# Grouped-query attention over a cache and a token mixer: ring loads in halves and another order of work at the layers' changes

## The chip, the cores and the metric

The kernel runs on one core of a Trainium2 chip. A core has a tensor engine (TensorE, PE in the profile, with its weight loads as PEld), a vector engine (VectorE, DVE), a scalar engine for activations (ScalarE, ACT), GpSimd (POOL) and SyncE (SP), which here issues nearly all transfers from the chip's memory to the core's SBUF. Each engine works through its own queue of instructions in order and waits on semaphores that other engines and transfers raise. Sums of matrix products gather in PSUM, in banks of 128 partitions by 512 float32.

The metric is the time of one execution on the device, in microseconds (us). Of the kernel before, three runs were taken; the number that counts is their median.

## The reference

Two layers, each a grouped-query attention block over a cache (one new token, batch of 2) and a token mixer. All is float32.

```python
B, Sq, D = 2, 1, 512
Hq, Hkv, Sk, Dh = 32, 8, 32768, 128        # 4 query heads share one K/V head
def _A_ref(x, k_cache, v_cache, wq, wo):
    q = (x @ wq).reshape(B, Sq, Hq, Dh).transpose(0, 2, 1, 3)
    ...
    scores = jnp.einsum("bhqd,bhkd->bhqk", q, k) * (Dh ** -0.5)
    p = _softmax(scores, axis=-1)
    o = jnp.einsum("bhqk,bhkd->bhqd", p, v)
    return o.transpose(0, 2, 1, 3).reshape(B, Sq, Hq * Dh) @ wo
def _B_ref(x, w1, b1, w2, b2):             # F = 1792
    h = _layernorm(x, axis=-1)
    u = _gelu(jnp.einsum("bsd,sf->bdf", h, w1) + b1)
    y = jnp.einsum("bdf,fs->bds", u, w2) + b2
    return y.transpose(0, 2, 1)
x = A_x
x = x + _A_ref(_layernorm(x), A_k_cache, A_v_cache, A_wq, A_wo)
x = x + _B_ref(_layernorm(x), B_w1, B_b1, B_w2, B_b2)
x = x + _A_ref(_layernorm(x), A_k_cache, A_v_cache, A_wq, A_wo)
x = x + _B_ref(_layernorm(x), B_w1, B_b1, B_w2, B_b2)
```

The K and V caches hold 32768 keys of 128 numbers for each of 2 x 8 pairs of batch and K/V head: 16 MB of K and 16 MB of V for a pair, read in both layers.

## The kernel before, in words

**Units and chunks.** A unit is one (layer, batch, K/V head); there are 32, numbered n in the order of the list `units` (lines 268 to 279). Each unit's K and V are read in 8 chunks of 4096 keys (c = 0 to 7), 2 MB each. In SBUF a chunk fills one *cell* of `mem`: 128 partitions of 16 KB (line 102). There are 13 cells and a rest. A K chunk is used in two parts of 8 tensor-engine products each (`k_chunk`, line 413, with 128 x 512 results in a PSUM tile `scores`; four chunks share one bank, so a unit has two "halves" of scores), a V chunk in two parts of 8 products (`v_chunk`, line 553, into the PSUM tile `acc`). Part 0 reads the first half of the cell, part 1 the second.

**Softmax of a unit.** `max_1` and `max_2` (lines 427 to 440) make the maxima over all scores, with one small product each; `turn_scores` transposes a half of the scores from PSUM into the SBUF tile S[0] or S[1]; ScalarE makes the exponentials, either head by head (`exponentials`, line 448) or, at the changes, a whole half after one vector operation (`exponentials_at_once`, lines 460 and 463). `denominators`, `out_0`, `out_1`, `out_2` turn the sums of V into the block's output rows (the tile `rows`, line 236).

**The order.** There is no scheduler: the chunks of all units stand in one list, `stream`, sorted by the keys of lines 845 to 855. For each entry the program emits its loads (`load_k`, `load_v`), then its products; everything else is hung onto points of this list by `at(time, function)` and emitted when that many chunks (or half chunks) have been emitted. So the times in the code are positions in each engine's queue, not clock times. V of unit n is interleaved with K of unit n + 1.

**Loads.** SyncE issues the loads in the order of the list; a load waits until the cell it fills has been read by the tensor engine. The transfers of one queue then run one after another. `spread` (line 163) chooses where a chunk of the ring goes: into a whole cell, if one is found with at least two cells of loads between its release and its use, or into two halves of cells, each loaded by itself (`half`, line 147).

**The changes of layer.** Most heads are run for both batches before the first layer ends; three heads are kept for the change (`RESIDENT`), and head 7 is the `keeper`: of its K, chunks 0, 1 and 2 stay in cells 0, 1 and 9 (`KEPT_K`), of its V chunks 1 to 7 (nearly all) in other cells (`KEPT`), from the unit of layer 0 to that of layer 1. There are two such changes, one for each batch: N1 = 13 (unit (0, 0, 7), the last of layer 0, batch 0) and N2 = 16 (unit (0, 1, 7)). Because so much is kept, the ring of free cells is short there: the cells 7 and 8, that is four halves.

At the change after unit n = N1 the following runs (the same at N2, with other numbers):

- V of unit 13 ends (time 226, `vend`). `out_0` to `out_2` and `take_rows` make its output row; `mix_1` and `mix_2` (line 639) bring it into a PSUM tile `bcast` and take its mean and deviation.
- Meanwhile K chunks 2 to 7 of unit 14 = (0, 1, 5) are run (chunks 0 and 1 were run earlier).
- `hidden_sum` (time 228) is the token mixer: 14 pairs of a gelu on ScalarE (line 778) and a multiply-add on VectorE (lines 793, 795). `mix_3` (time 230.5, between the two parts of chunk 6) sums it with one product (line 803), copies it (line 805, ScalarE) and takes statistics; `to_columns` (time 231, line 302) brings the row into columns and writes xnT, the next layer's normalised input (lines 305 and 307).
- `make_q` for unit 15 = (1, 0, 7): steps 0 and 1 are the four query products (line 338, two tensor-engine passes each), emitted between the parts of K chunk 7 (time 231.5); step 2 copies the query row (line 347), step 3 transposes it (line 351).
- The maxima of unit 14 at time 232 and 232.5, on both sides of part 0 of K chunk 0 of unit 15 (kept in its cell); exponentials at 232.5 and 233.
- From time 233 V chunks of unit 14 and K chunks of unit 15 alternate. Of these K chunks 0, 1 and 2 are resident and need no load.

Before the change of layer the maximum over a half of the scores is emitted right with the last product of that half (line 423).

## Time and profile before

| | us |
|---|---|
| runs | 2508.97, 2509.38, 2503.17 |
| median of the runs | 2508.97 |
| profiled execution, its own time | 2503.93 |
| span of that execution's instructions | 2502.1 |
| tensor engine busy with products | 1386.8 (55% of the span) |
| VectorE busy | 239.8 (10%) |
| ScalarE busy | 187.9 (8%) |
| mean granted clock of the tensor engine | 0.767 |

The profile is of one execution. Its page lists busy times by engine, the span in 40 equal slices (with the data rate of each slice and the granted clock of the tensor engine), the DMA queues, the chain of waits that ended last, and groups of like instructions. Other views used below: the timeline (start, duration, engine, line, operation, tiles, count; in brackets the idle time before it and what ended it), the instructions in windows of time (for each engine the busy time and the count, then the granted clock, DMA share and GB/s), and the instructions of one source line with the time from a load's issue to its landing. SPq is SyncE's queue, which issues the loads (line 136). Lines 413 and 553 are the products of K and V, with 8 of them to half a chunk.

### The profile page before, as it was taken

How to read it: one execution, taken by the hardware profiler on the slowest of the kernel's cores; microseconds unless marked ns; L12 is line 12 of the kernel's file. 1: busy time of each engine (PE TensorE's matmuls, PEld its weight loads, DVE VectorE, ACT ScalarE, POOL GpSimd, SP SyncE). 2: the span in 40 equal slices, each digit the busy share in tenths (PEclk: the TensorE clock that was granted, in tenths of full speed). 3: DMA queues.
4: the chain of work that ended last, by engine and by line, in shares of the span. 5: the costliest groups of instructions: out<-in, count | busy, mean ns of one | idle time of the engine just before them, and what ended most of it. 6: DMA issues, size and time to landing. Idle time of an engine off the chain costs nothing.

```text
span 2502.1 us, 20483 instructions
## 1 busy us (share of the span) xinstructions
PE 1386.8 (55%) x9270; PEld 372.1 (15%) x9270; DVE 239.8 (10%) x632; ACT 187.9 (8%) x554; POOL 4.9 (0%) x17
## 2 busy tenths in 40 slices
PE   4545554645445554667577675455546555456546
PEld 1111111111111111111121121111111111111112
DVE  0000000000000000004013110000000000010002
ACT  0000000000000000002012010000000000011002
POOL 0000000000000000000000000000000000000000
PEclk8777777877777777878797887777777777777778
DMA  9999999999999999999999999999999999999996
GB/s 419 435 433 432 432 432 432 433 436 428 434 429 432 433 427 435 429 425 372 427 427 399 409 427 436 432 434 433 432 433 429 433 432 433 433 432 428 434 433 287
DMA packets 33072, 1063.04 MB, mean 425 GB/s; under 512 B 3925, under 2 KB 3929, under 8 KB 4826
## 3 DMA queue, kind: packets, MB, share of 16 engines
q1 hardware_dynamic: 32696, 1061.70, 98.8%
q8 instruction: 73, 1.20, 0.2%
q14 instruction: 13, 0.11, 0.0%
q10 hardware_dynamic: 290, 0.04, 0.0%
HBM read 1061.72 MB, written 0.00 MB: 424 GB/s over the span
## 4 chain that ended last, share of the span: by engine, by line
DMA 73%; PE 25%; DVE 1%; issue 1%; ACT 0%; SPq 0%; POOL 0%; DVEq 0%; ACTq 0%
DMA mem<-in_v_dram 37%; DMA mem<-in_kt_dram 36%; PE scores L413 11%; PE acc L553 10%; PE kept L338 1%; DVE acc L795 1%; PE rows L236 1%; PE bcast L338 0%; PE small L437 0%; PE small L593 0%; PE small L584 0%; PE bcast L803 0%; PE kept L735 0%; PE small L431 0%; PE small L351 0%
## 5 line engine op out<-in xcount | busy, mean ns | idle before, releaser
L413 PE MATMUL scores<-mem,small_sb 128*32 128x512 f32 x4096 | 638.3, 740 | 610.0 <-DMA mem<-in_kt_dram 609.7
L553 PE MATMUL acc<-mem,S 128*16 128x512 f32 x4088 | 611.2, 736 | 455.0 <-DMA mem<-in_v_dram 453.7
L413 PEld LDWEIGHTS scores<-mem,small_sb 128*32 128x32 f32 x4096 | 149.4, 128 | 999.5 <-issue 889.8
L448 ACT ACTIVATE S<-S,small_sb 128x128 f32<-128x128 f32 x240 | 123.6, 519 | 2112.4 <-DVE small_sb L439 1644.8
L553 PEld LDWEIGHTS acc<-mem,S 128*16 128x16 f32 x4088 | 134.2, 110 | 826.3 <-issue 692.5
L423 DVE TENSOR_REDUCE small_sb<-scores 128x1 f32<-128x512 f32 x64 | 44.2, 691 | 915.5 <-PE scores L413 915.5
L443 DVE STREAM_TRANSPOSE S<-scores 128x512 f32<-128x512 f32 x64 | 45.4, 710 | 130.1 <-PE acc L553 130.1
L338 PE MATMUL kept<-mem,small_sb 128*2 128x512 f32 x104 | 51.0, 616 | 1.7 <-DVE small_sb L264 1.7
L236 PE MATMUL rows<-mem,small_sb 128*1 128x512 f32 (+1 forms) x276 | 48.8, 612 | 2.6 <-ACT mem L778 2.4
L448 ACT ACTIVATION_READ_ACCUMULATOR S<-S,small_sb 128x1 f32 x240 | 44.8, 187 | 0.0
L433 DVE TENSOR_REDUCE small_sb<-small 1x4 f32<-1x128 f32 x32 | 8.9, 279 | 277.8 <-PE small L431 277.8
L523 DVE SCALAR_TENSOR_TENSOR S<-acc,small_sb,S 128x128 f32<-128x128 f32 x93 | 32.6, 351 | 3.3
L586 DVE RECIPROCAL small_sb<-small 128x4 f32<-128x4 f32 x32 | 5.9, 184 | 281.8 <-PE small L584 281.8
L595 DVE TENSOR_TENSOR small_sb<-small,small_sb 128x4 f32<-128x4 f32 x31 | 5.1, 164 | 288.2 <-PE small L593 288.2
L778 ACT ACTIVATE S<-bcast,small_sb 128x512 f32<-128x512 f32 x28 | 21.5, 776 | 98.9 <-DVE small_sb L647 96.7
L351 PE MATMUL small<-small_sb,mem 2*128 2x2 f32 x112 | 14.8, 250 | 17.9 <-DVE mem L347 17.9
L521 DVE TENSOR_SCALAR S<-acc,small_sb 128x128 f32<-128x128 f32 x31 | 10.8, 348 | 112.9 <-PE acc L553 112.9
L593 PEld LDWEIGHTS small<-small_sb,S 128*128 128x128 f32 x62 | 12.2, 248 | 46.6 <-issue 41.5
L338 PE MATMUL bcast<-mem,small_sb 128*1 128x512 f32 (+1 forms) x40 | 18.5, 592 | 0.0
L795 DVE SCALAR_TENSOR_TENSOR acc<-S,small_sb,acc 128x512 f32<-128x512 f32 x24 | 18.1, 755 | 2.5
L351 PEld LDWEIGHTS small<-small_sb,mem 2*128 2x128 f32 x112 | 13.7, 188 | 30.5 <-DVE mem L347 27.3
L431 PE MATMUL small<-small_sb 128*1 128x128 f32 x64 | 16.7, 355 | 0.6 <-DVE small_sb L429 0.6
(134 smaller groups left out, 267.8 us busy)
## 6 DMA issues: line engine op xcount, KB each, us to landing
mem<-in_kt_dram SPq DMA_DIRECT2D x35, 2048.0 KB, 17.6
mem<-in_v_dram SPq DMA_DIRECT2D x27, 2048.0 KB, 21.4
mem<-in_v_dram SPq DMA_DIRECT2D x9, 4096.0 KB, 27.1
mem<-in_wqo_dram SPq DMA_DIRECT2D x14, 2048.0 KB, 33.2
mem<-in_kt_dram SPq DMA_DIRECT2D x7, 4096.0 KB, 24.1
mem<-in_kt_dram SPq DMA_DIRECT2D x18, 1024.0 KB, 7.6
mem<-in_v_dram SPq DMA_DIRECT2D x13, 1024.0 KB, 7.0
mem<-in_v_dram SPq DMA_DIRECT2D x2, 1280.0 KB, 26.5
```

Of the source, the lines that this page charges most:

```text
L236: nc.tensor.matmul(rows[32 * g : 32 * g + b + 1, :], weights if b else weights[:, 1:], row, start=False, stop=True, skip_group_check=True,)
L338: nc.tensor.matmul(q_ps[n][:m, :], xnT[:, d, b : b + m], wq_at(h)[:, d, :], start=(d == 0), stop=(d == DT - 1),)
L351: nc.tensor.matmul(pt[:, r * m : (r + 1) * m], q_row[n][:m, r * DH : (r + 1) * DH], ident[:m, :m], start=True, stop=True,)
L413: nc.tensor.matmul(sc_ps[n, half][32 * g : 32 * g + 32, :], q, kc[k * NG + g], start=(i == 0 and k == 0), stop=(i == PACK - 1 and k == SUB ...
L423: nc.vector.tensor_reduce(mx[n][:, half : half + 1], sc_ps[n, half], axis=AX.X, op=ALU.max)
L431: nc.tensor.matmul(pm[:1, :P], mxa, ident, start=True, stop=True)
L443: nc.vector.transpose(S[half], sc_ps[n, half])
L448: nc.scalar.activation(s[:, :, h], s[:, :, h], AF.Exp, bias=neg[n][:, h : h + 1], scale=SCALE, accum_out=lsum[n][:, half, h : h + 1],)
L523: nc.vector.scalar_tensor_tensor(t, acc[:, k * DH : (k + 1) * DH], mask[:, k : k + 1], t, op0=ALU.mult, op1=ALU.add)
L553: nc.tensor.matmul(acc[32 * g : 32 * g + R * QT, :], S[half][:, col : col + R * QT], vc[q], start=(c == 0 and q < NG), stop=(c == NCH - 1 ...
L778: nc.scalar.activation(hid[key, f], px[key], AF.Gelu_apprx_tanh, bias=shift[key][:, f : f + 1], scale=slope[key][:, f : f + 1],)
L795: nc.vector.scalar_tensor_tensor(h if f == FT - 1 else acc, h, w, acc, op0=ALU.mult, op1=ALU.add)
```

## The change

No operation is added to or removed from the computation. The edits:

- `spread` takes `parted`: K chunks 2 to 7 of the units N1 + 1 and N2 + 1 are always loaded as two halves, where chunks 2 and 3 had gone into whole cells.
- At the two changes `mix_2` moves from time vend + 1.5 to vend + 1 and `hidden_sum` from vend + 2 to vend + 1, so that both stand ahead of K chunk 3 of the unit (the chunk at vend + 1); `mix_3` from vend + 4.5 to vend + 5 (behind K chunk 6, no longer between its parts), `to_columns` from vend + 5 to vend + 5.5 (between the parts of K chunk 7). The maximum over the first half of that unit's scores becomes a function of its own, `highest`, and is emitted at vend + 4.5, behind the sum's work in VectorE's queue, no longer with K chunk 3.
- The query products become `q_products`: one product ahead of `max_1`, one between `max_1` and `max_2`, two behind the first exponentials; all at `kend` = vend + 6, ahead of V chunk 0. They had stood between the parts of K chunk 7.
- In `stream` the V chunks of the units N1 + 1 and N2 + 1 get keys two lower: V chunks 0 and 1 come first, then K chunk 0 of the next unit, then they alternate. So V ends two places earlier against K, and K chunks 0, 1 and 2, which are resident, each stand two V chunks later.
- What follows from the positions: in the ring of four halves (7.5, 8, 8.5, 7, in cells) now go K chunks 2 to 7 and V chunks 0 to 4 of the unit, where it had been K chunks 4 to 7 and V chunks 0 to 2 (at the second change some of the V halves go to cell 0). K chunk 3 of the next unit and all that follows are in whole cells as before; K chunk 6 of unit 19 is one whole cell, where it had been two halves.
- Unit 15's (and 18's) K ends one place later and its V begins where it did, so `max_2`, both halves of exponentials and V chunk 0 stand together, where K chunk 1 of unit 16 had stood between the maxima and V chunk 0.

```diff
--- before.py
+++ after.py
@@ -160,10 +160,10 @@
 
         return sum(brings[int(-(-a // 1)) : b])
 
-    def spread(until):
+    def spread(until, parted=False):
 
         k = min((*range(WCELL0 + 1), KEPT[3][1]), key=lambda k: (-fit(k, 1, until), idle(k)))
-        if fit(k, 1, until) >= 2:
+        if fit(k, 1, until) >= 2 and not parted:
             hold(k, 1, until)
             return [cells(k)]
         return [half(until - 0.5), half(until)]
@@ -320,6 +320,21 @@
         layer, b, h = unit_of(n)
         return units.index((layer, B - 1, h)) if b == 0 and (layer == 0 or h in passing) else None
 
+    def q_products(n, *ds):
+
+        layer, b, h = unit_of(n)
+        m = 1 if partner(n) is None else B
+        for d in ds:
+            if d == 0:
+                q_ps[n] = pfix.tile([P, 512], F32, name="bcast") if N1 < n <= N3 + 2 else kept[0]
+            nc.tensor.matmul(
+                q_ps[n][:m, :],
+                xnT[:, d, b : b + m],
+                wq_at(h)[:, d, :],
+                start=(d == 0),
+                stop=(d == DT - 1),
+            )
+
     def make_q(n, step, place=None):
 
 
@@ -330,18 +345,8 @@
             if step == 3:
                 nc.vector.tensor_copy(qpad[n % 2][:, 28 : 28 + R], q_kept.pop(n))
             return
-        if step == 0:
-
-            q_ps[n] = pfix.tile([P, 512], F32, name="bcast") if N1 < n <= N3 + 2 else kept[0]
         if step < 2:
-            for d in range(step * DT // 2, (step + 1) * DT // 2):
-                nc.tensor.matmul(
-                    q_ps[n][:m, :],
-                    xnT[:, d, b : b + m],
-                    wq_at(h)[:, d, :],
-                    start=(d == 0),
-                    stop=(d == DT - 1),
-                )
+            q_products(n, 2 * step, 2 * step + 1)
         if step == 2:
             q_row[n] = spot() if place is None else place
             nc.vector.tensor_copy(q_row[n][:m, :], q_ps[n][:m, :])
@@ -388,7 +393,7 @@
             hold(own, m, until)
             bufs = [cells(own, m)]
         elif limit == RING:
-            bufs = spread(until)
+            bufs = spread(until, n in (N1 + 1, N2 + 1) and c > 1)
         else:
             bufs = [buffer(m, limit, until)]
         src, f = piece(kt, b * HKV + h, c, m), 0
@@ -420,7 +425,12 @@
         if i == PACK - 1 and part == SUB - 1:
             if half == 0:
                 mx[n] = field(n, 0, HALVES)
-            nc.vector.tensor_reduce(mx[n][:, half : half + 1], sc_ps[n, half], axis=AX.X, op=ALU.max)
+            if half or n not in (N1 + 1, N2 + 1):
+                highest(n, half)
+
+    def highest(n, half):
+
+        nc.vector.tensor_reduce(mx[n][:, half : half + 1], sc_ps[n, half], axis=AX.X, op=ALU.max)
 
     m4, neg = {}, {}
 
@@ -848,7 +858,7 @@
             if n in (N1, N2):
                 key = (n + 1) * NCH + 1 + (c + 1) / (2 * NCH)
             elif n in (N1 + 1, N2 + 1):
-                key = (n + 1) * NCH - 0.5 + max(c / (2 * NCH) - 0.5, c + 1)
+                key = (n + 1) * NCH - 0.5 + max(c / (2 * NCH) - 0.5, c - 1)
             else:
                 key = (n + 1) * NCH + c + m - 1 + (LAG if N1 < n <= N3 else 0)
             stream.append((key, 1, n, c, m, limit))
@@ -879,16 +889,17 @@
         urgent = n in (N1, N2, NU - 1)
         if n:
             if n in (N1 + 2, N2 + 2):
-                q0 = q1 = q2 = mixed[layer - 1, b] + 0.5
-                q3 = q2 + 0.5
+                q2 = mixed[layer - 1, b]
+                q3 = q2 + 1
                 place = S[1]
             else:
                 place = S[0] if n in (N2 + 1, N3 + 1) else None
                 q0 = kbeg[n] - (10 if n == N3 + 1 else 6)
                 q1, q2, q3 = q0 + 1, q0 + 2, q0 + 2
             assert q3 <= kbeg[n]
-            at(q0, make_q, n, 0)
-            at(q1, make_q, n, 1)
+            if n not in (N1 + 2, N2 + 2):
+                at(q0, make_q, n, 0)
+                at(q1, make_q, n, 1)
             at(q2, make_q, n, 2, place)
             at(q3, make_q, n, 3, rank=int(q3 == q2))
             if place is S[0]:
@@ -896,13 +907,15 @@
         if n and (units[n] == (0, 0, h) or h in passing and units[n] == (1, 0, h)):
             at(kbeg[n] - 10, load_weights, h, (again if layer else weight_cell)[h])
         if n in (N1 + 1, N2 + 1):
-            t0 = mixed[units[n - 1][:2]]
-            at(t0, turn_scores, n, 0, rank=2)
+            at(kend - 0.5, turn_scores, n, 0, rank=2)
+            at(kend, q_products, n + 1, 0)
             at(kend, max_1, n)
-            at(kend + 0.5, max_2, n)
-            at(kend + 0.5, exponentials_at_once, n, 0)
-            t1 = kend + 1
-            assert t0 + 1 <= kend == kbeg[n + 1]
+            at(kend, q_products, n + 1, 1)
+            at(kend, max_2, n)
+            at(kend, exponentials_at_once, n, 0)
+            at(kend, q_products, n + 1, 2, 3)
+            t1 = kend + 2
+            assert mixed[units[n - 1][:2]] == kend == kbeg[n + 1] - 2
             at(t1, turn_scores, n, 1, rank=2)
             at(t1, exponentials_at_once, n, 1, rank=2)
             at(t1 + 1, sums, n)
@@ -937,15 +950,16 @@
             key = (layer, b)
             at(vend - 1 if change else vend, mix_1, key)
             at(vend + (1 if change else 2), take_rows, key, row_tile())
-            at(vend + (1.5 if change else 3), mix_2, key)
+            at(vend + (1 if change else 3), mix_2, key)
             at(vend + (0 if change else 1), gelu_table)
             if change:
 
                 assert k_done[n + 1, NCH - 1] == vend + 6
-                at(vend + 2, hidden_sum, key, rank=2)
-                at(vend + 4.5, mix_3, key)
-                at(vend + 5, to_columns, key)
-                mixed[key] = vend + 5
+                at(vend + 1, hidden_sum, key)
+                at(vend + 4.5, highest, n + 1, 0)
+                at(vend + 5, mix_3, key)
+                at(vend + 5.5, to_columns, key)
+                mixed[key] = vend + 6
             else:
```

## The prediction

> **What bounds the kernel now.** I read the page's parts on DMA first, then the stretches around the two layer changes, then their timeline.
>
> ```profile
> span 2502.1 us, 20483 instructions
> ...
> GB/s 419 435 433 432 432 432 432 433 436 428 434 429 432 433 427 435 429 425 372 427 427 399 409 427 436 432 434 433 432 433 429 433 432 433 433 432 428 434 433 287
> DMA packets 33072, 1063.04 MB, mean 425 GB/s; under 512 B 3925, under 2 KB 3929, under 8 KB 4826
> ...
> DMA 73%; PE 25%; DVE 1%; issue 1%; ACT 0%; SPq 0%; POOL 0%; DVEq 0%; ACTq 0%
> ```
>
> The transfers set the end: a slice of 62.6 us moves about 430 GB/s everywhere but in the first, the last and slices 19, 22 and 23. At 429 GB/s the 1063.04 MB take 2478 us of the 2502.1; about 24 us are lost, and the windows tell how much lies at the layer changes (the last two columns are DMA share and GB/s):
>
> ```profile
> 1140.00:1200.00 60.00, 42.37 (x268) 11.04 (x268) 24.24 (x47) 14.11 (x19) 1.08 (x2) 0.87 0.92 367
> 1200.00:1260.00 60.00, 36.88 (x222) 7.71 (x214) 4.84 (x13) 4.19 (x16) 0.00 (x0) 0.76 1.01 429
> 1340.00:1400.00 60.00, 45.27 (x280) 11.13 (x276) 24.95 (x48) 14.12 (x19) 1.08 (x2) 0.86 0.95 380
> 1400.00:1460.00 60.00, 37.66 (x222) 8.68 (x214) 4.85 (x13) 4.18 (x16) 0.00 (x0) 0.75 1.01 428
> ```
>
> (429 - 367)/429 x 60 = 8.7 us and (428 - 380)/428 x 60 = 6.7 us. Products that waited for a transfer date its landing more exactly:
>
> ```profile
> 1148.31 1.07 PE L413 MATMUL scores<-mem,small_sb 128*32 128x512 f32 x8 [1.42 <-DMA mem<-in_kt_dram]
> ...
> 1153.20 1.06 PE L413 MATMUL scores<-mem,small_sb 128*32 128x512 f32 x8 [1.66 <-DMA mem<-in_kt_dram]
> ...
> 1160.83 1.93 PE L413 MATMUL scores<-mem,small_sb 128*32 128x512 f32 x8 [1.60 <-DMA mem<-in_kt_dram]
> ...
> 1163.93 1.94 PE L413 MATMUL scores<-mem,small_sb 128*32 128x512 f32 x8 [1.17 <-DMA mem<-in_kt_dram]
> ...
> 1166.42 1.57 PE L413 MATMUL scores<-mem,small_sb 128*32 128x512 f32 x8 [0.56 <-DMA mem<-in_kt_dram]
> ...
> 1194.37 1.05 PE L553 MATMUL acc<-mem,S 128*16 128x512 f32 x8 [1.06 <-DMA mem<-in_v_dram]
> ...
> 1199.23 3.64 PE L413 MATMUL scores<-mem,small_sb 128*32 128x512 f32 x16 [3.80 <-DMA mem<-in_kt_dram]
> ...
> 1223.71 1.91 PE L553 MATMUL acc<-mem,S 128*16 128x512 f32 x16 [1.36 <-DMA mem<-in_v_dram]
> ```
>
> From 1199.23 to 1223.71 five cells (2 MB each) landed: 4.90 us a cell, 2.45 a half; the two halves at 1163.93 and 1166.42 lie 2.49 apart. From 1153.20 (K chunk 3 of unit 14) to 1199.23 (K chunk 3 of unit 15) eight cells landed: K 4 to 7, V 0 to 2, and that one. They are due in 39.2 us and took 46.0: **6.8 us lost at the first change**. At the second, in the chain of waits, K chunk 3 of unit 17 stands at 1348.35 and V chunk 4 at 1408.87; eleven cells (K 4 to 7, V 0 to 4, two K of unit 18) are due in 53.9 and took 60.5: **6.6 us lost**.
>
> ```profile
> 1348.35 1.07 PE scores L413 x8
> ...
> 1389.32 19.41 DMA mem<-in_v_dram
> 1408.87 3.65 PE acc L553 x16
> ```
>
> Where it goes is in the timeline of the first change:
>
> ```profile
> 1143.41 3.47 PE L553 MATMUL acc<-mem,S 128*16 128x512 f32 x16 [1.89 <-DMA mem<-in_v_dram]
> ...
> 1147.32 1.12 DVE L523 SCALAR_TENSOR_TENSOR S<-acc,small_sb,S 128x128 f32<-128x128 f32 x3
> ...
> 1150.50 1.04 PE L236 MATMUL rows<-mem,small_sb 128*1 128x512 f32 x8
> ...
> 1151.61 0.69 DVE L607 COPY S<-rows 128x512 f32<-128x512 f32 x1 [1.72 <-PE rows L236]
> ...
> 1154.19 1.12 PE L639 MATMUL bcast<-S,small_sb 128*128 128x512 f32 x2
> ...
> 1170.51 1.71 PE L803 MATMUL bcast<-S,small_sb 128*128 128x512 f32 x2 [2.51 <-DVE S L795]
> ...
> 1172.15 1.94 PE L413 MATMUL scores<-mem,small_sb 128*32 128x512 f32 x8
> 1172.26 0.60 ACT L805 ACTIVATE S<-bcast 128x512 f32<-128x512 f32 x1 [1.18 <-PE bcast L803]
> ...
> 1174.02 1.19 PE L302 MATMUL small<-small_sb,S 128*128 128x1 f32 x8
> ...
> 1175.38 0.27 DVE L307 TENSOR_SCALAR small_sb<-small,small_sb 128x4 f32<-128x4 f32 x1
> ...
> 1176.02 3.17 PE L338 MATMUL bcast<-mem,small_sb 128*1 128x512 f32 x7
> ...
> 1180.56 0.69 DVE L423 TENSOR_REDUCE small_sb<-scores 128x1 f32<-128x512 f32 x1 [0.23 <-PE scores L413]
> ...
> 1181.56 0.15 DVE L429 TENSOR_REDUCE small_sb<-small_sb 128x1 f32<-128x2 f32 x1
> ...
> 1184.96 1.91 PE L553 MATMUL acc<-mem,S 128*16 128x512 f32 x16 [0.65 <-ACT S L463]
> ...
> 1186.68 1.90 PE L413 MATMUL scores<-mem,small_sb 128*32 128x512 f32 x16
> ```
>
> The ring is two cells in halves. PE stands at L803 from 1168.0 (1166.42 + 1.57) to 1170.51 while a landed K half waits behind it, then works through mixer, queries, maxima and the resident K chunk of unit 15 before V chunk 0 at 1184.96. A half is loaded again only when PE has read it, so SyncE's queue stands too:
>
> ```profile
> 1186.07 0.33 SPq L136 DMA_DIRECT2D mem<-in_v_dram  x1
> ...
> DMA to landing us min/median/max: 4.6/7.5/23.3
> ...
> 1185.00:1190.00 5.00, 5.00 (x46) 1.50 (x50) 3.08 (x5) 0.63 (x1) 0.00 (x0) 1.00 0.60 206
> ...
> 1370.00:1375.00 5.00, 5.00 (x27) 1.33 (x26) 1.29 (x4) 0.00 (x0) 0.13 (x1) 1.00 0.93 290
> ```
>
> The load issued at 1186.07 is V chunk 2's first half, and 1185 to 1190 moves 206 GB/s. A load takes at least 4.6 us to land.
>
> **The change part by part.** No load and no operation is added; 14 more loads are halves (8 at each change, minus two of unit 19 that become one).
>
> *Entrance in halves.* K chunk 2 now lands in halves, the first at 1148.3 - 2.45 = 1145.9. PE is free at 1146.9 (1143.41 + 3.47), so its 8 products end at 1148.0. L593 waits for DVE's end at 1148.4, the second half's products end at 1150.0, and L236 at 1151.0 instead of 1151.5. SyncE waits here, in order, for each half; behind that wait stand only later loads of the ring, each released earlier than now.
>
> *The sum at the fifth chunk.* L639 now goes straight after L607's copy and no longer behind 8 products of chunk 3: 1151.0 + 0.1 + 0.7 = 1151.8 instead of 1154.19. PE waits those 0.8 us with chunk 3's first half landed; that lag is small against the ring's allowance below. L803 follows L639 by 16.3 us (1170.51 - 1154.19), so its input is ready at 1168.1. It now stands behind chunk 6's second half, which lands at 1153.2 + 6 x 2.47 = 1168.0 and ends by 1169.9 (1.94 at worst). **L803 waits for nothing, and no landed half stands behind it.** The maximum over the first scores (0.69 us of DVE) goes behind the sum; there DVE waits for L803 and the copy anyway; uncovered it would add its 0.7.
>
> *Queries in the wait.* L803 1169.9 to 1171.6; chunk 7's first half to 1172.7, while ACT's copy runs (0.60); L302 to 1173.9; second half, landed 1173.0, to 1175.0; one query product, 0.9 (two of eight passes in 3.2 to 3.5). DVE: L307 1.6 us after L302 starts, 1174.4; transpose 0.7, maximum 0.7, L429 at 1175.8. From L429 to the first V product it was 1184.96 - 1181.56 = 3.4 us, with resident K products in PE's gaps then and the other query products now. **V chunk 0 starts at about 1179.3 instead of 1184.96**, the 16 products of the resident chunk (1.9) and most of the query products being gone from its way.
>
> *Resident K behind two V.* V chunk 1 follows V chunk 0, with the query's transposes between (1.05). A half must be issued 4.6 us before it is due, and is due four halves (9.8 us) after the one it replaces: PE may read a half up to 5.2 us after its landing. V chunk 0's first half lands at 1153.2 + 9 x 2.47 = 1175.4 and is read by 1180.3: 4.9 us. This is the tightest; chunk 1 is read by 1183.5 and 1184.4, 3.1 and 1.6 behind. After that a pair of V and resident K costs PE 1.9 + 1.9 = 3.8 us against 4.9 a cell. At the second change the same steps leave a little more room (V chunk 0 at about 1374.4).
>
> *Four halves until V chunk 4.* Before, K chunk 3 of unit 15 went to a free cell as soon as SyncE passed V chunk 2, and two cells were then queued at once. Now V chunks 3 and 4 wait for ring halves ahead of it. With the lags above each is issued 6 to 8 us before it is due, so nothing is lost directly.
>
> *What is left.* The halves at 1163.93 (3.10 us after the one at 1160.83) and the stretch from 1370, share 0.93 but 290 GB/s, show that a queue nearly run dry restarts slowly: 0.65 us there, up to (0.93 x 429 - 290)/429 x 5 = 1.3 us here. Bounds for a change: 0 (all issued in time) and 4 (three such restarts). I take 1.2, two of the small kind, since the tight places are chunk 5 and V chunk 2. Spacing 2.47 to 2.49 instead of 2.45 for 8 more halves: 0.2.
>
> *Behind the changes.* Unit 15's exponentials now stand directly before its V chunk 0 with no K chunk between: four at 0.52, some 2.5 us of PE wait. That chunk lands 4.9 us after the K chunk before it, and two whole cells are queued behind; nothing, or 2.5 twice if that cover were gone.
>
> ```profile
> L448 ACT ACTIVATE S<-S,small_sb 128x128 f32<-128x128 f32 x240 | 123.6, 519 | 2112.4 <-DVE small_sb L439 1644.8
> ```
>
> Sum: (6.8 - 1.4) + (6.6 - 1.4) = **10.6 us regained**, bounds 5 and 13.4. The profiled execution took 2503.93 around its span of 2502.1: 2493.3. It lies 5.0 under the median of 2508.97, and the shown runs scatter over both; from the median it would be 2498.4. I forecast between, 2496.
>
> **The rivals.** *Halves cost more than half.* If each of the 14 added halves takes 3.1 us as at 1163.93 instead of 2.45, 9.1 us go back: 1.5 regained, 2502 (2507 from the median). For it: the slow rows above. Against: 2.49 when three halves are queued, which the new order keeps up. The Trainium skill ("DMA: Bandwidth & Descriptors", section Bandwidth) advises at least 1 MiB a DMA and gives 341 GB/s for 1 MB against 425 for 16 MB issued from GpSimd; by that an estimated 0.6 us more for each half. The trace's 2.49 us for a queued half disagrees.
>
> *PE becomes the bound: slower.* The granted clock halves when PE stands:
>
> ```profile
> 1200.00:1205.00 5.00, 3.75 (x24) 0.59 (x20) 0.69 (x1) 0.00 (x0) 0.00 (x0) 0.50 1.03 439
> ```
>
> There 16 products take 3.6 us (the row at 1199.23), a V and K pair 7.3 against 4.9. If that clock held through the whole change, PE's work between L803 and V chunk 0 (some 6.6 us at full clock beside L803) would double and V chunk 0 stand near 1185.9, so the old 6.8 us stay lost; the three pairs that now run on ring halves would lose 3 x 2.4 = 7.2 more: 14.4 over both changes, 2518. It decides once a pair exceeds 4.9 us. Against it: the clock is 1.00 from 1185 to 1190 in just such pairs. The Trainium skill ("TensorE: Matmul & The Clock Gate", Part 1: What's actually happening) has half rate after about 3.4 us idle and full rate after as long busy; by that, pairs that keep PE 78% busy could fall either way.
>
> *The wait only changes its name.* If the chain from maxima to exponentials keeps V chunk 0 near 1184.96, only the entrance gains (about 1 us a change): 2502. For it: the last 3.4 us of that chain are hand-overs between engines, which no order shortens. Against it: the resident chunk and six of the eight query passes are PE work that stood ahead of V chunk 0 and no longer do.
>
> **How the numbers follow.** Chances: forecast 0.63, halves cost more 0.20, PE the bound 0.09, name only 0.08. Likeliest alone: 2490.5 (all 13.4 from the profiled run) to 2502 (7 from the median). For eight in ten: 2490 to 2506, which takes in most of the second and fourth case. 0.3%, about what can be told, is 7.5 us: the forecast passes it nine times in ten, the second rarely. Faster 0.60, same 0.29, slower 0.11.
>
> **What would show it.** In the changed profile: L803's product with no wait for DVE, about 2 us earlier against the landing of chunk 3; V chunk 0 some 26 us after that landing (now 31.8); V chunk 2's first half issued 6 us earlier; no 5 us stretch near 206 GB/s; the 60 us windows at about 415. Wrong if the halves of V 2 to 4 land more than 2.6 us apart, if PE shows clock 0.5 with 7 us a pair there, or if a new gap appears behind unit 15's exponentials.

## The result, and the profile after

| | before | changed |
|---|---|---|
| median of six runs each, us | 2508.97 | 2494.39 |
| lowest to highest, us | 2503.17 to 2510.5 | 2493.08 to 2497.67 |
| profiled execution, its own time, us | 2503.93 | 2494.97 |
| span of that execution, us | 2502.1 | 2493.1 |

The changed kernel takes 0.9945 of the time before, with a 95% interval of 0.9933 to 0.9958: faster by more than the 0.3% that can be told. It is 14.6 us by the medians, and 9.0 by the two profiled spans.

The page of the changed kernel, with its data rates in 40 slices:

```profile
span 2493.1 us, 20496 instructions
...
GB/s 420 436 433 424 436 436 433 430 436 433 431 429 437 433 430 431 429 426 403 428 425 421 427 430 427 435 433 428 435 433 433 430 432 432 430 436 431 431 436 282
```

Most slices stand near 430 GB/s as before. Of those that fell behind, 19 now moves 403 GB/s (before 372), 22 moves 421 (399) and 23 moves 427 (409). The two windows of 60 us that hold the changes of layer, and one of 5 us (the last columns are granted clock, DMA share, GB/s):

```profile
1140.00:1200.00 60.00, 46.84 (x304) 11.63 (x296) 24.31 (x47) 14.12 (x19) 1.09 (x2) 0.87 0.99 402
1340.00:1400.00 60.00, 45.30 (x294) 11.39 (x290) 24.84 (x46) 14.12 (x19) 1.08 (x2) 0.93 1.01 421
...
1180.00:1185.00 5.00, 5.00 (x49) 1.90 (x44) 2.88 (x5) 0.63 (x1) 0.00 (x0) 1.00 0.88 339
```

By the prediction's reckoning, (429 - 402)/429 x 60 = 3.8 us are now lost in the first window and (428 - 421)/428 x 60 = 1.0 in the second, together 4.8 where it had been 8.7 + 6.7 = 15.4. The timeline of the first change shows the steps:

```profile
1145.90 1.07 PE L418 MATMUL scores<-mem,small_sb 128*32 128x512 f32 x8 [0.57 <-DMA mem<-in_kt_dram]
...
1149.25 1.04 PE L236 MATMUL rows<-mem,small_sb 128*1 128x512 f32 x8
1151.11 1.12 PE L649 MATMUL bcast<-S,small_sb 128*128 128x512 f32 x2 [0.81 <-DVE S L617]
...
1153.34 0.16 PEld L418 LDWEIGHTS scores<-mem,small_sb 128*32 128x32 f32 x8 [1.02 <-DMA mem<-in_kt_dram]
...
1168.56 1.94 PE L418 MATMUL scores<-mem,small_sb 128*32 128x512 f32 x8 [0.54 <-DMA mem<-in_kt_dram]
1170.43 2.07 PE L813 MATMUL bcast<-S,small_sb 128*128 128x512 f32 x2
...
1179.84 1.91 PE L563 MATMUL acc<-mem,S 128*16 128x512 f32 x16
...
1182.66 1.91 PE L563 MATMUL acc<-mem,S 128*16 128x512 f32 x16
1184.39 1.90 PE L418 MATMUL scores<-mem,small_sb 128*32 128x512 f32 x16
...
1189.55 1.66 PE L563 MATMUL acc<-mem,S 128*16 128x512 f32 x8 [2.40 <-DMA mem<-in_v_dram]
...
1199.40 1.05 PE L563 MATMUL acc<-mem,S 128*16 128x512 f32 x8 [0.76 <-DMA mem<-in_v_dram]
1204.30 1.94 PE L418 MATMUL scores<-mem,small_sb 128*32 128x512 f32 x8 [3.85 <-DMA mem<-in_kt_dram]
```

Lines 418, 563, 649 and 813 are what lines 413, 553, 639 and 803 were. K chunk 3 of unit 14 landed by 1153.34 (the weight load of its second half waited for it), K chunk 3 of unit 15 by 1204.30; ten cells lie between now (K 4 to 7, V 0 to 4 and that one), due in 49.0 us at 4.90 each. They took 51.0: 2.0 us lost, before 6.8. L813 runs straight behind the product ahead of it, with no bracket for DVE. V chunk 0 starts at 1179.84. SyncE's queue issues V chunk 2's first half right after:

```profile
1180.96 0.33 SPq L136 DMA_DIRECT2D mem<-in_v_dram  x1
```

The second change, from chunk 3 of unit 17 to chunk 3 of unit 18, again ten cells:

```profile
1342.97 0.29 PEld L418 LDWEIGHTS scores<-mem,small_sb 128*32 128x32 f32 x8 [0.56 <-DMA mem<-in_kt_dram]
...
1368.10 1.91 PE L563 MATMUL acc<-mem,S 128*16 128x512 f32 x16
...
1392.81 1.92 PE L418 MATMUL scores<-mem,small_sb 128*32 128x512 f32 x16 [1.02 <-DMA mem<-in_kt_dram]
```

1392.81 - 1342.97 = 49.8 us for 49.0: 0.8 lost, before 6.6. Both measures say the same: 13.4 - 2.8 by landings and 15.4 - 4.8 by data rates are each 10.6 us regained at the changes. Two questions are left for experiments: which part carries it, and why the medians moved by four microseconds more.

### The profile page after: what moved, and what is told of

It reads as the page before. It is cut to its first block, busy times and chain, and to the rows that moved or that the text cites. A ratio compares the mean times of both kernels' runs of the same rounds, so it can differ in the third digit from the quotient of the medians.

```text
span 2493.1 us, 20496 instructions
## 1 busy us (share of the span) xinstructions
PE 1378.2 (55%) x9270; PEld 369.7 (15%) x9270; DVE 240.1 (10%) x632; ACT 187.9 (8%) x554; POOL 4.9 (0%) x17
## 4 chain that ended last, share of the span: by engine, by line
DMA 74%; PE 24%; issue 0%; DVE 0%; ACT 0%; SPq 0%; POOL 0%
DMA mem<-in_v_dram 39%; DMA mem<-in_kt_dram 35%; PE scores L418 11%; PE acc L563 11%; PE kept L330 1%; PE rows L236 1%; PE bcast L330 1%; PE small L603 0%; PE small L447 0%; PE small L594 0%; PE kept L745 0%; PE small L441 0%; PE bcast L813 0%; PE small L356 0%; SPq L136 0%
## 5 line engine op out<-in xcount | busy, mean ns | idle before, releaser
L418 PE MATMUL scores<-mem,small_sb 128*32 128x512 f32 x4096 | 629.9, 732 | 615.9 <-DMA mem<-in_kt_dram 615.8
L236 PE MATMUL rows<-mem,small_sb 128*1 128x512 f32 (+1 forms) x276 | 48.6, 617 | 2.6 <-ACT mem L788 2.4
```

Of the source, the lines that this page charges most:

```text
L236: nc.tensor.matmul(rows[32 * g : 32 * g + b + 1, :], weights if b else weights[:, 1:], row, start=False, stop=True, skip_group_check=True,)
L418: nc.tensor.matmul(sc_ps[n, half][32 * g : 32 * g + 32, :], q, kc[k * NG + g], start=(i == 0 and k == 0), stop=(i == PACK - 1 and k == SUB ...
```

## The experiments

In the table, "lost" is worked out from the GB/s of the two windows as above, so it belongs to the one execution that was profiled, which need not be the median one (2502.12 us for `queries_back`, 2499.53 for `whole_entrance`). The ratio is to runs of the kernel before on the same chip; the medians come from several chips, on which that kernel's median was 2507.07 to 2508.97. A kernel without a ratio ran once.

| kernel | median, us | ratio, 95% interval | GB/s at the changes | lost, us |
|---|---|---|---|---|
| changed | 2494.39 | 0.9945 [0.9933, 0.9958] | 402, 421 | 4.8 |
| after_again | 2493.91 | 0.9942 [0.9927, 0.9957] | 408, 421 | 3.9 |
| mixer_back | 2495.32 | 0.9958 [0.9943, 0.9972] | 409, 407 | 5.7 |
| whole_entrance | 2498.09 | 0.9958 [0.9942, 0.9975] | 384, 405 | 9.5 |
| queries_back | 2503.75 | 0.9991 [0.9982, 1.0001] | 378, 385 | 13.2 |
| v_order_back | 2503.83 | 0.9991 [0.9982, 1.0001] | 379, 385 | 13.0 |
| v_later | 2501.48 | 0.9973 [0.9962, 0.9985] | 378, 394 | 11.9 |
| ring_split | 2496.28 | 0.9952 [0.9937, 0.9967] | 403, 420 | 4.8 |
| sum_between | 2493.62 | 0.9946 [0.9929, 0.9963] | 407, 408 | 5.9 |
| warm | 2493.69 | 0.9944 [0.9928, 0.9960] | 407, 421 | 4.1 |
| warm_between | 2494.55 | 0.9949 [0.9930, 0.9969] | 410, 415 | 4.5 |
| before_again | 2504.94 | | 356, 385 | 16.2 |
| before_third | 2509.61 | | 338, 363 | 21.8 |

**The mixer's order undone.** The maximum over the first scores, the row's entrance, the fourteen pairs and the sum go back to their old places, the rest of the change stays.

```diff
-                at(vend + 1, hidden_sum, key)
-                at(vend + 4.5, highest, n + 1, 0)
-                at(vend + 5, mix_3, key)
-                at(vend + 5.5, to_columns, key)
+                at(vend + 2, hidden_sum, key, rank=2)
+                at(vend + 4.5, mix_3, key)
+                at(vend + 5, to_columns, key)
```

`mix_2` goes back to vend + 1.5, and `highest` is emitted with chunk 3 again.

> The changed kernel with the mixer's places of before at both changes (statistics behind the first part of K chunk 3, the sum behind chunk 3, its last product between the parts of chunk 6, the maximum over the first scores with chunk 3). Theory (a ring half may be read up to 5.2 us after its landing, and only V chunk 0 comes near): with the entrance in halves the sum's last product would be ready near 1169.8, within a microsecond of where the changed kernel has it (1170.4), and the second half of chunk 6 is read 4 us behind its landing; V chunk 0 starts 0 to 1 us later, 0 to 2 us are lost over both changes: 2494.5 to 2497. Rival (the sum at the fifth chunk is what regains the time): 2.4 us at each change are given back, 2499 or more.

The median is in the range expected. The first window is no worse than the changed kernel's, and V chunk 0 starts at 1178.42 there, 1.4 us earlier, where 0 to 1 us later was expected; the second window loses about 2 us more. The medians are 0.9 us apart and the intervals overlap. The timeline of its second change:

```profile
1354.86 1.93 PE L418 MATMUL scores<-mem,small_sb 128*32 128x512 f32 x8 [0.56 <-DMA mem<-in_kt_dram]
...
1360.18 1.85 PE L418 MATMUL scores<-mem,small_sb 128*32 128x512 f32 x8
```

From 1356.79 to 1360.18 no product of K runs: the sum, back between the two parts of chunk 6, holds up a half. The old wait is there, and it costs little beside the other parts of the change. What the mixer's order is worth by itself is between nothing and some 2 us.

**The queries undone.** They go back between the parts of K chunk 7; their transposes come ahead of the maxima.

```diff
-                q2 = mixed[layer - 1, b]
-                q3 = q2 + 1
+                q0 = q1 = q2 = mixed[layer - 1, b] - 0.5
+                q3 = q2 + 0.5
...
-            at(kend, q_products, n + 1, 0)
             at(kend, max_1, n)
-            at(kend, q_products, n + 1, 1)
             at(kend, max_2, n)
             at(kend, exponentials_at_once, n, 0)
-            at(kend, q_products, n + 1, 2, 3)
```

> The changed kernel with all four query products between the parts of K chunk 7, as before, and the transposes of the query ahead of the maxima. Theory (ring lag): 3.4 us of products and 1 us of transposes stand ahead of the second part of chunk 7 and of the maxima; V chunk 0 starts about 4 us later than the 1179.8 of the changed kernel, its first half is read some 9 us behind its landing where 5.2 are allowed, and each change loses 3 to 5 us: 2500 to 2504. Rival (those products are covered by waits between the engines either way): V chunk 0 moves under 1 us, 2494 to 2496.

Timeline of its first change:

```profile
1173.77 3.16 PE L330 MATMUL bcast<-mem,small_sb 128*1 128x512 f32 x7 [0.88 <-DVE small_sb L307]
...
1182.30 5.32 PE L563 MATMUL acc<-mem,S 128*16 128x512 f32 x32 [1.64 <-ACT S L473]
```

PE waits for L307, does seven of the eight query passes ahead of the last scores, and at the end waits 1.64 us for the exponentials (L473), with nothing left to fill the wait: V chunk 0 at 1182.30 instead of 1179.84. That is 2.5 us later, where about 4 were expected, but the time came in the range: by the medians 9.4 of the 14.6 us go, and against the kernel before on the same chip (2507.07) 3.3 us of the gain are left.

**The order of V undone.** Resident K and V alternate from the start again.

```diff
-                key = (n + 1) * NCH - 0.5 + max(c / (2 * NCH) - 0.5, c - 1)
+                key = (n + 1) * NCH - 0.5 + max(c / (2 * NCH) - 0.5, c + 1)
```

with `q3 = q2` and `t1 = kend + 1` to suit.

> The changed kernel with V and resident K in the order of before: resident K chunk 0 of the next unit ahead of V chunk 0, so that the query's transposes stand ahead of V too, and the four halves only to V chunk 2. Theory (ring lag): 1.1 us of transposes, 0.7 of the copy they wait for and 1.9 of the resident chunk come ahead of V chunk 0, which starts near 1183.6 instead of 1179.8; 2.5 to 4.5 us are lost at each change: 2499 to 2503. Rival (two whole cells queued early, K chunk 3 and V chunk 3, make up for the later V chunk 0): 2494 to 2496.

Timeline of its first change:

```profile
1180.90 1.92 PE L418 MATMUL scores<-mem,small_sb 128*32 128x512 f32 x16 [0.26 <-DVE small_sb L364]
1182.64 1.90 PE L563 MATMUL acc<-mem,S 128*16 128x512 f32 x16
```

The resident chunk stands ahead of V chunk 0 and waits for the query's last copy; V chunk 0 comes at 1182.64, a microsecond earlier than expected, and yet 9.4 us are given back, 0.8 more than the range expected. With either part undone the ratio is 0.9991, within 0.3% of no change. The two do not add (9.4 and 9.4 are more than 14.6): they are needed together.

**V chunk 0 later, and nothing else.** To see whether the time of V chunk 0 is the cause, 14 pairs of small products whose result nothing reads (they are in the kernel's last stage anyway) are put ahead of it.

```diff
             at(kend, q_products, n + 1, 2, 3)
+            at(kend, idle_products, 14)
```

> The changed kernel with 14 more products of the identity with itself on the tensor engine ahead of V chunk 0 at each change (their result is not used): some 4 to 5.6 us of work, by 28 passes of 0.145 to 0.2 us. Theory (ring lag): the first half of V chunk 0 is read 4.9 us behind its landing in the changed kernel, so nearly each microsecond added is a microsecond lost at both changes, plus a slow restart: 8 to 12 us over both, 2502 to 2507. Rival (the tensor engine, 55% busy, makes it up behind V chunk 0): 2494 to 2497.

```profile
1179.15 3.39 PE L693 MATMUL small<-small_sb 128*128 128x128 f32 x28
1182.47 1.91 PE L563 MATMUL acc<-mem,S 128*16 128x512 f32 x16
...
1207.23 1.08 PE L418 MATMUL scores<-mem,small_sb 128*32 128x512 f32 x4 [3.84 <-DMA mem<-in_kt_dram]
```

In this timeline of its first change V chunk 0 starts 2.63 us later than in the changed kernel and K chunk 3 of unit 15 lands 2.93 later (1207.23 against 1204.30). The two windows lose 7.1 us more, the medians 7.1; the added products took 3.39 us and not 4 to 5.6, so the median lies just under the range expected. So the changed kernel stands at the edge of the ring's allowance: a microsecond of lateness of V chunk 0 costs about one, or somewhat more, at each change.

**Whole cells at the entrance.** Chunks 2 and 3 go into whole cells where one is found; the order of work is the changed one.

```diff
-            bufs = spread(until, n in (N1 + 1, N2 + 1) and c > 1)
+            bufs = spread(until)
```

> The changed kernel without the entrance in halves: K chunks 2 and 3 of the units at the changes go into whole cells as before, the order stays the changed one. Theory (ring lag): chunk 2 is read from its whole landing at 1148.3 instead of 1145.9, the first loads of chunk 4 issue 2 to 2.5 us later, the sum starts later by the same, its last product is ready near 1168 to 1169 and still stands behind chunk 6; V chunk 0 moves by under 1 us and 1 to 3 us are lost over both changes, mostly as slow landings of chunks 4 and 5 as in the kernel before: 2495 to 2498. Rival (the four halves at the entrance carry the gain): 2500 or more.

Timeline of its first change:

```profile
1155.48 1.12 PE L649 MATMUL bcast<-S,small_sb 128*128 128x512 f32 x2 [0.82 <-DVE S L617]
1156.54 3.64 PE L418 MATMUL scores<-mem,small_sb 128*32 128x512 f32 x32
1162.67 1.06 PE L418 MATMUL scores<-mem,small_sb 128*32 128x512 f32 x8 [2.49 <-DMA mem<-in_kt_dram]
1166.35 1.94 PE L418 MATMUL scores<-mem,small_sb 128*32 128x512 f32 x8 [2.62 <-DMA mem<-in_kt_dram]
...
1182.55 1.91 PE L563 MATMUL acc<-mem,S 128*16 128x512 f32 x16
```

Chunk 2 lands as a whole and the row's work starts later, so L649 runs at 1155.48 instead of 1151.11. Chunk 3 stands behind L649 now, and is read together with chunk 4 from 1156.54 (x32). Its cell is loaded again that much later, and chunk 5's halves come at 1162.67 and 1166.35. V chunk 0 then starts at 1182.55, 2.7 us later than in the changed kernel, where under 1 was expected; that is as late as in `v_later`, and the first window loses about as much (6.3 us against 7.1). In all 4.7 us are given back by the windows and 3.7 by the medians (the intervals overlap), just past the upper end of the range expected. That the mixer ahead of chunk 3 is only cheap with the entrance in halves is a reading of this timeline; no run undid both.

**Many more halves.** Every whole cell that `spread` hands out is loaded in two halves: 35 more loads, the order of work unchanged.

```diff
-            return [cells(k)]
+            return [cells(k)[:, : CK // 2], cells(k)[:, CK // 2 :]]
```

> The changed kernel with every whole cell of the ring loaded as two halves of the same cell: 35 more loads of half the size, in the same order, each half waiting for less. It measures what a half costs when it is issued early. Theory (a queued half costs 0.02 to 0.04 us more than half a cell): 0.7 to 1.4 us, 2494 to 2497. Rival (a half costs 0.6 us more than half a cell, as the late ones at 1163.93 do): 21 us, 2515.

The page's line of K's halves (x24 in the changed kernel), then the timeline behind the first change:

```profile
mem<-in_kt_dram SPq DMA_DIRECT2D x74, 1024.0 KB, 16.0
```

```profile
1227.32 1.91 PE L563 MATMUL acc<-mem,S 128*16 128x512 f32 x8 [0.56 <-DMA mem<-in_v_dram]
1229.79 1.91 PE L563 MATMUL acc<-mem,S 128*16 128x512 f32 x8 [0.57 <-DMA mem<-in_v_dram]
1232.28 1.86 PE L418 MATMUL scores<-mem,small_sb 128*32 128x512 f32 x8 [0.59 <-DMA mem<-in_kt_dram]
```

Halves land 2.47 and 2.49 us apart. At 0.65 us for each added load (the rival's price) 35 of them would cost 22.8 us; the median is 1.9 above the changed kernel's, with overlapping intervals. The rival falls. The Trainium skill ("DMA: Bandwidth & Descriptors", section Bandwidth) gives 341 GB/s for 1 MB issued from GpSimd; a half here is 1.05 MB in 2.48 us, 423 GB/s, when others are queued with it, so the measurement decides against that price.

**The clock held, the sum between the parts.** In `warm`, three pairs of the unread products stand behind each of five half chunks ahead of the sum; `sum_between` puts the sum between the parts of chunk 6; `warm_between` does both.

```diff
+                for k in (2.5, 3, 3.5, 4, 4.5):
+                    at(vend + k, idle_products, 3, rank=2)
```

```diff
-                at(vend + 5, mix_3, key)
-                at(vend + 5.5, to_columns, key)
+                at(vend + 4.5, mix_3, key)
+                at(vend + 5, to_columns, key)
```

> The changed kernel with 3 products of the identity with itself behind each part of K chunks 4, 5 and the first of 6 at both changes (result not used), in the tensor engine's waits for landings. Theory (granted clock: the parts of chunk 6 take 1.93 us and the sum's last product 2.07, where 1.07 and 1.12 are seen at full clock): the clock stays up, V chunk 0 starts 1 to 2 us earlier and is read within its allowance; about 1 us less is lost: 2492 to 2494, and a shorter part of chunk 6 in the profile. Rival (the added products delay the reading of the ring): a part is read over 5.2 us behind its landing and 1 to 4 us are lost: 2495 to 2498.

> The changed kernel with the sum's last product between the parts of K chunk 6 again (its input is ready there at 1167.4, before the second part lands at 1168.5) and the step to columns behind chunk 6. Theory (the tensor engine's own work sets V chunk 0 now, not the hand-overs): V chunk 0 starts 0.5 to 1 us earlier, 0 to 1 us less is lost at the first change, where 2.1 us are left: 2492.5 to 2494.5, not to be told from the changed kernel. Rival (a product ahead of landed K parts costs what it cost before): 2496 or more.

> Both of the last two together. Theory: V chunk 0 starts 1.5 to 2.5 us earlier than in the changed kernel, and the first change loses about 1 us instead of 2.1: 2492 to 2493.5. Rival: as for each alone, 2495 or more.

> The changed kernel, unchanged, beside the other three on one chip: 2494 to 2496, and a profile with about 2 us lost at the first change and 1 us at the second, as in the first one. If the ordinary loss is another (a restart that is slow by chance), it shows in these two places.

The first change in `warm`, timeline (PE, then SyncE's queue):

```profile
1169.46 1.12 PE L813 MATMUL bcast<-S,small_sb 128*128 128x512 f32 x2
...
1178.70 1.91 PE L563 MATMUL acc<-mem,S 128*16 128x512 f32 x16
...
1189.91 1.05 PE L563 MATMUL acc<-mem,S 128*16 128x512 f32 x8 [1.08 <-DMA mem<-in_v_dram]
```

```profile
1179.82 0.33 SPq L136 DMA_DIRECT2D mem<-in_v_dram  x1
```

L813 takes 1.12 us instead of 2.07, and V chunk 0 starts 1.14 earlier; V chunk 2's load is issued 1.14 earlier; yet its second half, issued at 1180.67 instead of 1181.81, lands by 1189.91, no earlier than the 1189.55 of the changed kernel. `sum_between` has V chunk 0 at 1178.49 and the same late half:

```profile
1178.49 1.91 PE L563 MATMUL acc<-mem,S 128*16 128x512 f32 x16
...
1183.18 1.05 PE L563 MATMUL acc<-mem,S 128*16 128x512 f32 x8 [0.82 <-DMA mem<-in_v_dram]
...
1189.49 1.05 PE L563 MATMUL acc<-mem,S 128*16 128x512 f32 x8 [2.69 <-DMA mem<-in_v_dram]
```

The medians of these three and of the changed kernel (2494.39, and 2493.91 in `after_again`, which ran on one chip with `whole_entrance`, `v_later` and `ring_split`) lie within 1 us, and no version beats the changed kernel by a difference that can be told. `warm` and `sum_between` lie in their ranges, `after_again` 0.1 us under its own; `warm_between`, at 2494.55, missed it by a microsecond. `sum_between` also shows where the sum's new place helps: its second window loses 1.8 us more than the changed kernel's, with L813 there waiting 1.43 us for the sum, as in `mixer_back`.

The 2 us still lost at the first change are thus not PE's lateness. Most of them lie in the transfers around 1185: in `sum_between` the second half of V chunk 1 landed by 1183.18 and that of V chunk 2 by 1189.49, 6.31 us for two halves that are due in 4.9. What makes these transfers slow was not found.

**Before, twice more.** One execution each, to see how much the loss at the changes differs from one to the next.

> The kernel before, unchanged: its profiled execution took 2503.93 us, 5 us under the median of its runs (2508.97), and the question is where an ordinary execution loses the other 5 us. If those 5 us are lost in the rings of four halves (loads issued too late, so that landings restart slowly), the windows 1140 to 1200 and 1340 to 1400 move less than the 367 and 380 GB/s of the profile shown, together by about 5 us x 429 GB/s, and an ordinary execution of the changed kernel regains them too: then the term of the sum was too small. If they are lost elsewhere (start, tail, or everywhere by a lower rate), those windows stay at 367 and 380 and the span is longer in another place.

> The kernel before, unchanged, once more with a profile: its first change lost 6.9 us in one profiled execution and 9.5 in another. If restarts that are slow by chance make the spread of its runs, the loss at the first or second change differs again by 1 to 3 us while the rest of the span stays within 1.5 us; if the two profiles differ by something else, both changes stay near 6.9 and 6.6.

`before_again` took 2504.94 us, about as little as the profile of the prediction, so it could not say where the other 5 us go. Its first change was still slower than that profile's (10.2 us lost in the window against 8.7): the granted clock from 1150 to 1155 was 0.51 instead of 1.00, and L803 and V chunk 0 came 1.2 and 1.3 us later.

`before_third` took 2509.61 us, near the median of this kernel's runs. Its windows:

```profile
1140.00:1200.00 60.00, 46.22 (x272) 12.33 (x264) 24.29 (x47) 14.13 (x19) 1.09 (x2) 0.81 0.88 338
1340.00:1400.00 60.00, 45.51 (x268) 12.71 (x264) 24.30 (x47) 14.14 (x19) 1.08 (x2) 0.82 0.90 363
...
1175.00:1180.00 5.00, 5.00 (x17) 1.86 (x18) 1.03 (x3) 0.00 (x0) 0.00 (x0) 0.50 0.83 264
```

and its timeline of the first change, with the start of V at the second:

```profile
1170.50 2.08 PE L803 MATMUL bcast<-S,small_sb 128*128 128x512 f32 x2 [1.58 <-DVE S L795]
...
1177.88 4.28 PE L338 MATMUL bcast<-mem,small_sb 128*1 128x512 f32 x7
...
1187.93 1.91 PE L553 MATMUL acc<-mem,S 128*16 128x512 f32 x16 [0.65 <-ACT S L463]
...
1368.63 2.08 PE L803 MATMUL bcast<-S,small_sb 128*128 128x512 f32 x2 [2.85 <-DVE S L795]
...
1385.98 1.91 PE L553 MATMUL acc<-mem,S 128*16 128x512 f32 x16 [0.65 <-ACT S L463]
```

L803 starts when it did in the prediction's profile (1170.50 against 1170.51). But the granted clock then stays at 0.50 from 1175 to 1180, so seven query passes take 4.28 us instead of 3.17, a part of K chunk 7 ahead of them 1.93 instead of 1.07 and L302 1.87 instead of 1.19, and V chunk 0 comes 17.4 us after L803 instead of 14.5. At the second change it is 17.4 again, instead of 14.4. So V chunk 0 is some 3.0 us later at each change; the windows lose 4.1 and 2.4 us more (21.8 in all against 15.4 of the prediction's profile), and the spans differ by 5.7. In the same 5 us the profile before and the changed one have the clock at 1.00:

```profile
1175.00:1180.00 5.00, 5.00 (x26) 1.23 (x26) 1.39 (x4) 0.00 (x0) 0.00 (x0) 1.00 0.98 372
```

```profile
1175.00:1180.00 5.00, 4.81 (x24) 1.09 (x20) 2.70 (x7) 0.63 (x1) 0.00 (x0) 1.00 1.01 401
```

(first the kernel before, then the changed one.)

**All profiles side by side.** At the first change, the start of V chunk 0, the landing of V chunk 2's second half (as the product that waited for it shows it) and the loss in the window from 1140 to 1200:

| kernel | V chunk 0 at | second half of V chunk 2 by | lost, us |
|---|---|---|---|
| warm_between | 1178.38 | 1189.44 | 2.7 |
| mixer_back | 1178.42 | 1189.42 | 2.8 |
| sum_between | 1178.49 | 1189.49 | 3.1 |
| warm | 1178.70 | 1189.91 | 3.1 |
| after_again | 1179.26 | 1189.55 | 2.9 |
| changed | 1179.84 | 1189.55 | 3.8 |
| ring_split | 1179.90 | 1189.81 | 3.6 |
| queries_back | 1182.30 | 1192.09 | 7.1 |
| v_later | 1182.47 | 1192.02 | 7.1 |
| whole_entrance | 1182.55 | 1193.52 | 6.3 |
| v_order_back | 1182.64 | 1192.30 | 7.0 |
| before | 1184.96 | 1194.37 | 8.7 |
| before_again | 1186.24 | 1196.90 | 10.2 |
| before_third | 1187.93 | 1198.21 | 12.7 |

Up to about 1179.9 the landing does not depend on V chunk 0; from 1182.3 on it follows 9.4 to 11.0 us behind it, whether query passes, a resident chunk, unread products, a late entrance or a low clock made it late. The changed kernel stands near the bend.

## Why the prediction was right, and where a term was off

2496 was forecast, 2494.39 came, inside the range, by the mechanism named. Step by step:

*Entrance in halves.* Chunk 2's first half at 1145.90, as worked out; L236 ended at 1150.29 (1149.25 + 1.04), 0.7 us earlier than the 1151.0 put down for its end, and L649 started after a wait of 0.81 for the copy, as expected, at 1151.11 for 1151.8. The step's worth was mis-sized: "only the entrance gains (about 1 us a change)" stands in the last rival, and undoing it under the new order costs 4.7 us by the windows, since V chunk 0 is then late as well. "No load and no operation is added" is not exact: the 14 halves stand for seven whole chunks, so seven more loads are issued.

*The sum at the fifth chunk.* L813 waits for nothing: right. It started at 1170.43 for 1169.9, because chunk 6's second half came at 1168.56 and not at 1168.0; its products took the 1.94 put down as the worst. As a gain of its own this is the smallest part: `mixer_back` is 0.9 us above by the medians, with overlapping intervals.

*Queries, and resident K behind two V.* V chunk 0 at 1179.84 for 1179.3, 26.5 us behind chunk 3's landing for 26. Chunk 1 was read by 1184.4 as put down, and V with resident K ran as pairs of 1.9 and 1.9, but for one K chunk of 2.70. That this was "the tightest" is shown: 2.6 us later costs 7 over both changes, 1.1 us earlier brings nothing that can be told.

*Four halves until V chunk 4.* V chunk 2's first half was issued at 1180.96 instead of 1186.07, 5.1 us earlier for 6. From its second half at 1189.55 to V chunk 4's at 1199.40 four halves took 9.85 us, 2.46 each: no sign of the 2.6 that would have spoken against it.

*What is left.* 1.4 us a change were put down for slow restarts; 2.0 and 0.8 were measured, 2.8 in all, as forecast. That it agrees so closely is partly chance: the two changes differ, the windows of the same execution say 4.8, and those of `after_again` 3.9.

*Behind the changes.* The exponentials of unit 15 did not delay its V chunk 0. The changed kernel's timeline there, PE and then ScalarE:

```profile
1253.82 2.79 PE L563 MATMUL acc<-mem,S 128*16 128x512 f32 x16 [2.76 <-DMA mem<-in_v_dram]
```

```profile
1252.81 0.50 ACT L458 ACTIVATE S<-S,small_sb 128x128 f32<-128x128 f32 x1
```

This is the fourth exponential; it ended at 1253.3, and the product started at 1253.82 with its transfer.

*The sum.* 10.6 us regained was forecast, and between the two profiled executions 10.6 were regained at the changes. The spans differ by 9.0 only; where the other 1.6 us lie was not found.

*The step that was off* is the last, from the profiled execution to the median: "6.8 us lost at the first change" and "6.6 us lost at the second" were taken for every run, and the 10.6 then set against either level, 2493.3 or 2498.4. But the loss is what the runs of the kernel before differ in. The one run near 2509 that was profiled loses some 6 us more at the changes (before_third, 21.8 against 15.4), and the changed kernel does not seem to inherit that: its six runs lie from 2493.08 to 2497.67, with their median 1.1 us above the 2493.3 worked out for the profiled execution. By the medians 14.6 us were regained, where 13 were forecast and 10.6 worked out. So the midpoint 2496 came close by luck: it was a compromise between two levels and had no mechanism of its own. The better reading is that the new order removes most of what makes the runs differ. That the other runs near 2509 have the same cause is argued from one of them, and why the changed kernel is spared was not tested.

*The rivals.* Halves that cost more: refuted by ring_split for halves that are queued early, and in the ring by the 2.46 us above. PE as the bound: the clock was at 0.50 from 1165 to 1170, just ahead of L813 (2.07 us), but 1.00 from 1180 to 1185, where V chunk 1 and the first resident chunk begin, and 0.99 from 1185 to 1190; its mechanism, work ahead of V chunk 0 at half clock, does exist, in the kernel before, where it made before_third slower. The wait only changing its name: that is what queries_back and v_order_back each do (0.9991, and V chunk 0 near 1182.5), so it was one edit away.

## What to carry to other kernels

Where transfers set the end and a short ring feeds them, ask how late the tensor engine may read a slot before the next load goes out too late, and bring every reader within that; here work that was earlier than the allowance brought nothing more, and two edits that each missed it alone looked nearly worthless until both were made. Load a slot in the pieces in which it is read when work stands between the pieces. And before a difference is set against a profile, look at how far the runs of the kernel scatter: if the stretch that the change touches is what scatters, the gain is to be reckoned from the usual run, and the result may be one level and not a shift.

## What the runs showed of the hardware

- **The clock of one stretch differs between executions of one program.** The same 5 us of the same order of work had a granted clock of 1.00 in one execution (before) and 0.50 in another (before_third). With the products slow at the second change too (seven query passes in 4.20 us instead of 3.17), V chunk 0 came 3.0 us later at each, and the span was 5.7 us longer. The Trainium skill ("TensorE: Matmul & The Clock Gate", Part 1: What's actually happening) has a free-running window behind the gate, so that the same kernel turns to full rate at different points, and puts the penalty under 1% of a span. This case agrees with the size, 5.7 of 2508 us being 0.2%, and with the same kernel turning at different points; no run here shows the window itself. Small as it is, 5.7 us is a good part of the 14.6 in question.
- **Issued earlier, landed no earlier.** `warm` issued both halves of V chunk 2 1.14 us earlier than the changed kernel did, and the second landed no earlier. In `warm` the 5 us from 1180 show the DMA engines nearly always busy (0.98) at only 375 GB/s:

```profile
1180.00:1185.00 5.00, 4.05 (x32) 1.44 (x28) 3.34 (x5) 0.63 (x1) 0.00 (x0) 0.85 0.98 375
```

For each byte the engines were busy some 10% longer there than in the prediction's window from 1200 to 1260 (1.01 at 429 GB/s); the changed kernel's 0.88 at 339 gives the same. Why is open.
